# Three more expert matrices loaded in halves inside the attention, and five loaded ahead of the slots d0 to d4

## The chip, the cores and the metric

The kernel runs on one core of one Trainium2 chip. The engines are PE (matrix multiply, with its weight loads shown apart as PEld), DVE (vector), ACT (scalar), POOL (general purpose) and SP, which here does nothing but issue DMAs. The 16 DMA engines of the core carry every transfer, and the code of the engines too. The metric is the device time of one execution in microseconds (us).

## The reference

```python
# attention in chunks of 64 over q, k, v of shape (8, 8, 576, 64)
scores = scale * np.matmul(q_c, k_c.transpose(0, 1, 2, 4, 3))
attn = softmax(scores); out = np.matmul(attn, v_c)
x = out.transpose(0, 2, 1, 3).reshape(4608, 512)
# soft mixture of experts: 8 experts with 4 slots each
logits = x @ phi                                  # (4608, 32)
slot_input = softmax_over_tokens(logits).T @ x    # (32, 512)
h = np.maximum(slot_input[e] @ w1[e], 0.0)        # w1: 8 x 512 x 1024
slot_out[e] = h @ w2[e]                           # w2: 8 x 1024 x 512
x = softmax_over_slots(logits) @ slot_out         # (4608, 512)
# two-layer network
h = x @ w_in                                      # w_in: 512 x 2048
out = softplus(h) @ w_out                         # w_out: 2048 x 512
```

## The kernel before, in words

The work has three stretches. In the **attention** (about the first 175 us) 36 units, each of two heads and 512 tokens, go through the steps A (transposes of q and k on PE), B and M (copies on ACT and POOL), S (scores), m0, m1, x (softmax), C and Ce (transpose of P), D (times v), n0, n1 (normalise) and E; after every fourth unit the steps F add the unit's tokens to the slot inputs (`acc`). In the **transition** (about 175 to 240 us) PE multiplies the slot inputs with w1 in the sixteen steps H, one for each half of an expert's matrix, then with w2 in the sixteen steps SO, while the other engines prepare the combine weights (steps c1 to d) and split w_in and w_out into two parts (steps cb to cl). In the **network** (the rest) PE runs the two layers over tiles of 256 tokens.

All steps are put in order when the program is built: `issue` plays a list of steps with costs, ranks and buffers, and calls each step's function in the order that comes out. Every engine then runs its instructions in that order, and semaphores make an instruction wait for what it needs. SP issues all loads in order too. A load of q and k for unit u (step lq) waits until PE has finished the transposes of unit u - 3, because there are three buffers for raw q and k.

Each of w1 and w2 comes as sixteen matrices of 1 MB. `W1` and `W2` give the SBUF slot of each: the slots w0 to w7 hold a matrix as two halves, a and b, of 512 KB; g0 to g3, i0 to i3 and d0 to d4 hold it in one piece of 1 MB. The slots d0 to d4 lie where the attention keeps its buffers, so that these five loads wait for the last A (d0), the last S (d1, d2) and the last D (d3, d4). PE uses the w1 matrices in the order w0, w1, g0, g1, g2, d0 to d4, w2 to w6, g3, and the first five w2 matrices are those in i0 to i3 and w7. Two of the later SO steps have extra matmuls ahead of them that only fill time:

```python
FILL = {("SO", 14): 4, ("SO", 15): 3, ("o", 0): 2}
...
    ends = ((raw_ctx, "A1", ["d0"]), (qk_ctx, "S", ["d1", "d2"]), (v_ctx, "D", ["d3", "d4"]))
```

The functions that the change touches:

Of the kernel before, what the change touches and what calls it, by code (L numbers as in the profile page):

```python
# [17 lines left out]
LAG = 3  # L18
BUSY = 36
WAIT = 0  # L20
FILL = {("SO", 14): 4, ("SO", 15): 3, ("o", 0): 2}


# [2 lines left out]
W2 = ["i0", "i1", "i2", "i3", "w7", "w0", "w1", "w2", "w3", "w4", "w5", "w6", "g3", "i0", "i1",  # L26
      "i2"]
# [117 lines left out]
def kernel(  # L145
# [12 lines left out]
    nc = tc.nc  # L158
# [40 lines left out]
    wt = {}  # L199
# [11 lines left out]
    def slot(sl, dt=F32):  # L211
        return pools[home(sl)].tile([128, 2048], dt, tag=sl, name=sl)


    def half_slot(sl, i, dt=F32):
        nm = sl + "ab"[i]
        return pools[home(sl)].tile([128, 1024], dt, tag=nm, name=nm)

    def halves(sl):
        if sl[0] == "w":  # L220
            return [half_slot(sl, i) for i in range(2)]
        t = V["slot", sl] = slot(sl)
        return [t[:, 0:1024], t[:, 1024:2048]]
# [62 lines left out]
    def load(nm, n, sl):  # L286


        e, i = divmod(n, 2)
        if nm == "w1":  # L290
            src = moe_w1[e].rearrange("(p k) f -> p k f", k=4)[:, 2 * i:2 * i + 2]
        elif nm == "w2":
            src = moe_w2[e, i * 512:(i + 1) * 512, :].rearrange("(p b a) f -> p b (a f)", b=2, a=2)
        else:
            src = w_out_u[256 * n:256 * n + 256, :].rearrange("(k p) f -> p k f", p=128)
        parts = halves(sl)
        if sl[0] == "w":
            for t, x in zip(parts, (src[:, 0], src[:, 1])):
                nc.sync.dma_start(out=t.bitcast(U32) if nm == "wo" else t, in_=x)
        else:  # L300
            t = V["slot", sl]
            t = (t.bitcast(U32) if nm == "wo" else t).rearrange("p (b f) -> p b f", b=2)
            for x in (slice(0, 1), slice(1, 2)) if nm == "w2" and n >= 14 else (slice(0, 2),):
                nc.sync.dma_start(out=t[:, x], in_=src[:, x])
        if nm == "w2":
            parts = [t.rearrange("p (a f) -> p a f", a=2) for t in parts]
        wt[nm, n] = parts

    def load_wi(c, pr):
        src = w_in_u[256 * pr:256 * pr + 256, 1024 * c:1024 * c + 1024].rearrange(  # L310
            "(k p) f -> p k f", p=128)
        sl = WI[c][0][pr]
        parts = halves(sl)
        if sl[0] == "w":
            for i in range(2):
                nc.sync.dma_start(out=parts[i].bitcast(U32), in_=src[:, i])
        else:
            nc.sync.dma_start(
                out=V["slot", sl].bitcast(U32).rearrange("p (b f) -> p b f", b=2), in_=src)
        wt["wi", c, pr] = parts  # L320
# [297 lines left out]
    def add(nm, key, fn, deps=(), take=(), give=(), rank=0.0, cost=None, after=()):  # L618
        s = Step(nm, key, fn, [by[d] for d in deps if d in by], take, give, rank, cost,
                 [by[d] for d in after])  # L620
        by[nm, key] = s
        steps.append(s)

    for u in range(NU):
# [4 lines left out]
            cost={"SP": 2.4} if G == MIXED else None)  # L629
# [27 lines left out]
        n = HP - 1 if G == NG - 1 else 0  # L657
# [61 lines left out]
    def at(f, *a):  # L719
        return lambda e, held: f(*a)  # L720

    for n, sl in enumerate(W1):
        if sl[0] != "d":
            add("lw", ("w1", n), at(load, "w1", n, sl), rank=100 + n)
    for n in range(5):
        add("lw", ("w2", n), at(load, "w2", n, W2[n]), rank=130 + n)
    ends = ((raw_ctx, "A1", ["d0"]), (qk_ctx, "S", ["d1", "d2"]), (v_ctx, "D", ["d3", "d4"]))
    deps = []
    for i, (c, nm, sls) in enumerate(ends):
        add("close", i, at(lambda c, sls: (c.close(), [open_pool(sl) for sl in sls]), c, sls),  # L730
            deps + [(nm, k) for k in range(NU)])
        deps = [("close", i)]
        for sl in sls:
            n = W1.index(sl)
            add("lw", ("w1", n), at(load, "w1", n, sl), deps, rank=110 + n)
# [14 lines left out]
    for a in range(4):  # L750
        sl = slice(32 * a, 32 * a + 32)
# [3 lines left out]
    for a in range(4):  # L755
        sl = slice(32 * a, 32 * a + 32)
# [3 lines left out]
        out=phi, in_=moe_phi.rearrange("(k p) s -> p k s", p=128)), rank=2.5)  # L760
# [151 lines left out]
    def fill(key, t):  # L912
        for _ in range(FILL.get(key, 0)):
            nc.tensor.matmul(
                out=t[:, 0:256], lhsT=ident, rhs=acc[:, 0:256], start=True, stop=True)
# [277 lines left out]
    for nm, n in AFTER:  # L1193
        r += 1
        if nm == "wi":
            for pr in range(2):
                sl = WI[n][0][pr]
                k = ("wi", n, pr)
                add("lw", k, at(load_wi, n, pr), (), [(sl, ("wi", n))], (), r, {"SP": 2.65}, prev)
                prev = [("lw", k)]  # L1200
        else:
            sl = W2[n] if nm == "w2" else f"w{n}"
            add("lw", (nm, n), at(load, nm, n, sl), (), [(sl, nm + str(n))], (), r, None, prev)
            prev = [("lw", (nm, n))]
    for n in range(16):
        key = "w2" if n < 5 else f"w2{n}"
# [59 lines left out]
    for a, b in pieces[0]:  # L1266
        k = (0, a)
# [8 lines left out]
    for c in range(4):  # L1276
# [4 lines left out]
        n, d = need[c]  # L1281
# [21 lines left out]
    for n in range(NQ):  # L1303
# [6 lines left out]
        for i, p in enumerate(ps):  # L1310
            k = (n, p[0])
            f, l = i == 0, i == len(ps) - 1
# [56 lines left out]
    for s in steps:  # L1369
# [12 lines left out]
        if s.nm in ("cb0", "cx0") and s.key[:2] == ("wi", 1):  # L1382
            s.after = [*s.after, by["mx", (WAIT, 0)]]

# [31 lines left out]
```

## Time and profile before

| what | before |
|---|---|
| median of 3 runs | 679.87 us (679.12 to 679.99) |
| the profiled execution | 677.97 us, its span 676.2 us |
| PE busy | 634.6 us, 94% of the span |
| DVE, ACT, POOL busy | 430.2, 318.0, 237.8 us |
| DMA | 107.93 MB, mean 160 GB/s |

The span runs from the first to the last instruction that was recorded; 1.77 us of the execution lie outside it. A difference between two kernels is a difference of whole times. PE's busy share shows that whatever makes PE wait is the time to look for; a wait of another engine counts only where PE waits for it in turn.

### The profile page before, as it was taken

How to read it: one execution, taken by the hardware profiler on the slowest of the kernel's cores; microseconds unless marked ns; L12 is line 12 of the kernel's file. 1: busy time of each engine (PE TensorE's matmuls, PEld its weight loads, DVE VectorE, ACT ScalarE, POOL GpSimd, SP SyncE). 2: the span in 40 equal slices, each digit the busy share in tenths (PEclk: the TensorE clock that was granted, in tenths of full speed). 3: DMA queues.
4: the chain of work that ended last, by engine and by line, in shares of the span. 5: the costliest groups of instructions: out<-in, count | busy, mean ns of one | idle time of the engine just before them, and what ended most of it. 6: DMA issues, size and time to landing. Idle time of an engine off the chain costs nothing.

```text
span 676.2 us, 14087 instructions
## 1 busy us (share of the span) xinstructions
PE 634.6 (94%) x5849; PEld 511.6 (76%) x5849; DVE 430.2 (64%) x631; ACT 318.0 (47%) x478; POOL 237.8 (35%) x205
## 2 busy tenths in 40 slices
PE   5899899878995899999999999999999999999997
PEld 4688678756454677888788788888888888888885
DVE  1678778765237799878887877754555554545551
ACT  2566457543126587734554755544333333333330
POOL 4233233220114536613222233444433344433341
PEclk7999999998897999999999999999999999999999
DMA  9799889899999903112313510222414223231412
GB/s 169 195 245 275 234 235 287 212 300 413 416 409 411 391 5 128 59 63 93 125 63 118 195 62 32 79 78 79 110 62 125 63 85 103 78 110 63 121 35 62
DMA packets 80543, 107.93 MB, mean 160 GB/s; under 512 B 42464, under 2 KB 60896, under 8 KB 78560
## 3 DMA queue, kind: packets, MB, share of 16 engines
q1 hardware_dynamic: 80480, 107.04, 49.0%
q8 instruction: 46, 0.75, 0.5%
q14 instruction: 17, 0.14, 0.1%
HBM read 88.15 MB, written 18.87 MB: 158 GB/s over the span
## 4 chain that ended last, share of the span: by engine, by line
PE 81%; DVE 8%; issue 4%; ACT 3%; POOL 2%; DMA 1%; SPq 1%; POOLq 0%; DVEq 0%; ACTq 0%
PE trm L1146 18%; PE trm L1144 18%; PE trm L1142 18%; PE ph L1084 5%; PE tr L404 4%; PE X L487 3%; PE S L435 2%; PE hps L931 2%; PE tr L468 2%; PE tr L522 2%; PE tr L540 2%; PE tr L598 1%; DMA q<-in_q_dram 1%; DVE nm L446 1%; DVE ph L1113 1%
## 5 line engine op out<-in xcount | busy, mean ns | idle before, releaser
L1123 POOL TENSOR_TENSOR g<-hTm,g 128x1024 fp32r<-128x1024 f32 (+1 forms) x37 | 86.8, 2348 | 105.1 <-ACT g L1119 101.5
L1109 ACT ACTIVATE hTm<-hTm 128x1024 f32<-128x1024 f32 (+2 forms) x51 | 51.4, 1010 | 79.8 <-DVE hTm L1103 79.6
L1103 DVE TENSOR_SCALAR hTm<-ph 128x1024 uint32<-128x1024 uint32 (+2 forms) x51 | 59.0, 1158 | 34.6 <-PE ph L1084 34.5
L421 POOL COPY T<-T 64x512 f32<-64x512 f32 x72 | 44.0, 611 | 104.3 <-ACT T L413 103.5
L1113 DVE SCALAR_TENSOR_TENSOR hTm<-ph,hTm 128x1024 f32<-128x1024 f32 (+1 forms) x37 | 44.1, 1193 | 23.5 <-ACT hTm L1109 23.4
L1119 ACT CAST g<-hTm 128x1024 fp32r<-128x1024 f32 (+1 forms) x37 | 37.9, 1025 | 41.0 <-DVE hTm L1113 41.0
L1158 DVE TENSOR_TENSOR i<-trm,i 128x512 f32<-128x512 f32 x52 | 35.7, 686 | 32.0 <-PE trm L1146 31.8
L413 ACT COPY T<-tr 128x512 f32<-128x512 f32 x72 | 40.9, 588 | 29.5 <-PE tr L404 29.4
L1084 PEld LDWEIGHTS ph<-cT,Tc 128*128 128x128 f32 x288 | 43.6, 190 | 10.1 <-issue 2.8
L1084 PE MATMUL ph<-cT,Tc 128*128 128x256 f32 x288 | 47.0, 286 | 0.8 <-DVE ph L1113 0.7
L1103 DVE TENSOR_SCALAR siT<-ph 128x1024 uint32<-128x1024 uint32 (+1 forms) x25 | 29.5, 1180 | 26.0 <-PE ph L1084 26.0
L1123 POOL TENSOR_TENSOR g<-siT,g 128x1024 fp32r<-128x1024 f32 x12 | 28.9, 2407 | 42.8 <-ACT g L1119 42.8
L1109 ACT ACTIVATE siT<-siT 128x1024 f32<-128x1024 f32 (+1 forms) x25 | 25.7, 1026 | 36.8 <-DVE siT L1103 36.6
L1123 DVE TENSOR_TENSOR g<-ph,g 128x1024 fp32r<-128x1024 f32 (+2 forms) x27 | 29.7, 1102 | 11.9 <-ACT g L1119 11.9
L446 DVE TENSOR_REDUCE nm<-S 128x8 f32<-128x512 f32 x36 | 24.7, 686 | 18.9 <-PE S L435 18.8
L404 PE MATMUL tr<-ident,q 128*128 128x128 f32 x144 | 29.8, 290 | 6.3 <-DMA q<-in_q_dram 5.2
L1119 ACT CAST g<-ph 128x1024 fp32r<-128x1024 f32 (+2 forms) x27 | 24.9, 922 | 19.5 <-DVE ph L1113 18.1
L435 PEld LDWEIGHTS S<-T 64*64 64x64 f32 x1152 | 21.1, 137 | 16.1 <-issue 12.5
L435 PE MATMUL S<-T 64*64 64x64 f32 x1152 | 25.4, 225 | 7.5 <-issue 2.5
L404 PE MATMUL tr<-ident,k 128*128 128x128 f32 x144 | 28.9, 283 | 2.2 <-issue 2.2
L460 ACT ACTIVATE P<-P 128x512 f32<-128x512 f32 x36 | 23.0, 638 | 11.5 <-DVE P L452 11.4
L452 DVE TENSOR_TENSOR P<-S,nm 128x512 f32<-128x512 f32 x36 | 24.5, 679 | 2.1 <-PE S L435 1.3
(439 smaller groups left out, 1748.4 us busy)
## 6 DMA issues: line engine op xcount, KB each, us to landing
part<-i SPq DMA_DIRECT2D x18, 512.0 KB, 2.6
i<-part SPq DMA_DIRECT2D x18, 512.0 KB, 3.7
q<-in_q_dram SPq DMA_DIRECT2D x32, 256.0 KB, 4.7
k<-in_k_dram SPq DMA_DIRECT2D x32, 256.0 KB, 4.4
vbm<-in_v_dram SPq DMA_DIRECT2D x40, 128.0 KB, 4.2
g<-in_moe_w_dram SPq DMA_DIRECT2D x5, 1024.0 KB, 7.6
d<-in_moe_w_dram SPq DMA_DIRECT2D x5, 1024.0 KB, 12.1
i<-in_moe_w_dram SPq DMA_DIRECT2D x5, 1024.0 KB, 15.2
```

Of the source, the lines that this page charges most:

```text
L404: nc.tensor.transpose(c, t[:, h, 2 * rr:2 * rr + 2, :].rearrange("p r d -> p (r d)"), ident)
L421: nc.gpsimd.tensor_copy(out=t[a:a + 64, :, 1], in_=t[b:b + 64, :, 2 * h])
L435: nc.tensor.matmul(out=sp[64 * o:64 * o + 64, b, 64 * i:64 * i + 64], lhsT=cs[:, 0], rhs=cs[:, 1], start=True, stop=True)
L1084: nc.tensor.matmul(out=ph(n, a, b)[:, j - a, :], lhsT=K["Tc"][:, f * 128:(f + 1) * 128], rhs=K["cT"][:, t * TT:(t + 1) * TT], start=True, ...
L1103: nc.vector.tensor_scalar(out=scratch(n, a, b).bitcast(U32), in0=ph(n, a, b).bitcast(U32), scalar1=0x80000000, scalar2=None, op0=ALU.bitwi ...
L1109: nc.scalar.activation(out=y, in_=y, func=AF.Softplus)
L1113: nc.vector.scalar_tensor_tensor(out=soft(n, a, b), in0=ph(n, a, b), scalar=0.0, in1=y, op0=ALU.max, op1=ALU.add)
L1119: nc.scalar.copy(out=V["gs", n][:, 0, a:b], in_=soft(n, a, b))
L1123: tt(e)(out=s[:, 1, a:b], in0=soft(n, a, b), in1=s[:, 0, a:b].bitcast(F32), op=ALU.subtract)
L1142: nc.tensor.matmul(out=po, lhsT=s[:, 0, j, ts_], rhs=wr[:, hs], start=(n in begin and j == 0), stop=False)
L1144: nc.tensor.matmul(out=po, lhsT=s[:, 0, j, ts_], rhs=wr[:, ls], start=False, stop=False)
L1146: nc.tensor.matmul(out=po, lhsT=s[:, 1, j, ts_], rhs=wr[:, hs], start=False, stop=(j == 3 and n in finish))
```

## The change

Three w1 matrices, those of the slots w2, w3 and w4, no longer load after the last q and k. Each is loaded as two halves, and each half is issued straight behind q and k of one unit: units 8, 10, 12, 21, 26 and 31. The five w2 matrices of i0 to i3 and w7 are issued ahead of those of d0 to d4 instead of behind them. The steps that carried these loads stay in the list, with their cost and without their load, so that the planner's order for PE, DVE, ACT and POOL is what it was.

```diff
+EARLY_LOADS = {10: (8, 10), 11: (12, 21), 12: (26, 31)}
...
+    def load_half(n, sl, i):
+        src = moe_w1[n // 2].rearrange("(p k) f -> p k f", k=4)[:, 2 * (n % 2) + i]
+        if i == 0:
+            wt["w1", n] = halves(sl)
+        nc.sync.dma_start(out=wt["w1", n][i], in_=src)
+
...
+    def ahead(key, f, step):
+        add("ld", key, f, cost={None: 0.0}, after=[step])
+
     for n, sl in enumerate(W1):
         if sl[0] != "d":
-            add("lw", ("w1", n), at(load, "w1", n, sl), rank=100 + n)
+            add("lw", ("w1", n), at(lambda: None) if n in EARLY_LOADS else at(load, "w1", n, sl),
+                rank=100 + n)
+        for i, u in enumerate(EARLY_LOADS.get(n, ())):
+            ahead((n, i), at(load_half, n, sl, i), ("lq", u))
     for n in range(5):
-        add("lw", ("w2", n), at(load, "w2", n, W2[n]), rank=130 + n)
+        add("lw", ("w2", n), at(lambda: None), rank=130 + n)
+        ahead(("w2", n), at(load, "w2", n, W2[n]), ("lw", ("w1", 15)))
```

On SP, the first place is the loads of units 8 to 12. In the rows of before, q_586 and k_587 are those of unit 8, q_634 and k_635 of unit 9, and so on; vbm and vb2 take v, four DMAs for two units.

```order
L265 DMA q_586<-in_q_dram 128x2x256
L265 DMA k_587<-in_k_dram 128x2x256
L265 DMA q_634<-in_q_dram 128x2x256
L265 DMA k_635<-in_k_dram 128x2x256
L272 DMA vbm_115<-in_v_dram 128x4x64 x4
L265 DMA q_733<-in_q_dram 128x2x256
L265 DMA k_734<-in_k_dram 128x2x256
L265 DMA q_768<-in_q_dram 128x2x256
L265 DMA k_769<-in_k_dram 128x2x256
L272 DMA vb2_116<-in_v_dram 128x4x64 x4
```

The same place on SP in the changed kernel, whose lines stand one lower; L314 is the load of a half.

```order
L266 DMA q_586<-in_q_dram 128x2x256
L266 DMA k_587<-in_k_dram 128x2x256
L314 DMA w2a_590<-in_moe_w1_dram 128x1024
L266 DMA q_637<-in_q_dram 128x2x256
L266 DMA k_638<-in_k_dram 128x2x256
L273 DMA vbm_115<-in_v_dram 128x4x64 x4
L266 DMA q_736<-in_q_dram 128x2x256
L266 DMA k_737<-in_k_dram 128x2x256
L314 DMA w2b_591<-in_moe_w1_dram 128x1024
L266 DMA q_772<-in_q_dram 128x2x256
L266 DMA k_773<-in_k_dram 128x2x256
L273 DMA vb2_116<-in_v_dram 128x4x64 x4
```

Two halves have come between the loads of units 8 to 11; a third, w3a, follows behind unit 12.

The second place on SP is the loads of units 26 to 28 and the whole matrix g1 behind them, before the change.

```order
L265 DMA q_2103<-in_q_dram 128x2x256
L265 DMA k_2104<-in_k_dram 128x2x256
L265 DMA q_2135<-in_q_dram 128x2x256
L265 DMA k_2136<-in_k_dram 128x2x256
L272 DMA vbm_115<-in_v_dram 128x4x64 x4
L265 DMA q_2239<-in_q_dram 128x2x256
L265 DMA k_2240<-in_k_dram 128x2x256
L304 DMA g1_2271<-in_moe_w1_dram 128x2048
```

The same loads on SP after the change.

```order
L266 DMA q_2111<-in_q_dram 128x2x256
L266 DMA k_2112<-in_k_dram 128x2x256
L314 DMA w4a_2115<-in_moe_w1_dram 128x1024
L266 DMA q_2146<-in_q_dram 128x2x256
L266 DMA k_2147<-in_k_dram 128x2x256
L273 DMA vbm_115<-in_v_dram 128x4x64 x4
L266 DMA q_2250<-in_q_dram 128x2x256
L266 DMA k_2251<-in_k_dram 128x2x256
L305 DMA g1_2282<-in_moe_w1_dram 128x2048
```

The half w4a now stands behind unit 26, ahead of all that follows.

The third place on SP is the end of the attention, from the load of g3 on, before the change.

```order
L304 DMA g3_3235<-in_moe_w1_dram 128x2048
L304 DMA d0_3270<-in_moe_w1_dram 128x2048
L304 DMA d1_3287<-in_moe_w1_dram 128x2048
L304 DMA d2_3316<-in_moe_w1_dram 128x2048
L304 DMA d3_3324<-in_moe_w1_dram 128x2048
L304 DMA d4_3326<-in_moe_w1_dram 128x2048
L304 DMA i0_3328<-in_moe_w2_dram 128x2048
L304 DMA i1_3330<-in_moe_w2_dram 128x2048
L304 DMA i2_3332<-in_moe_w2_dram 128x2048
L304 DMA i3_3334<-in_moe_w2_dram 128x2048
L299 DMA w7a_3336<-in_moe_w2_dram 128x1024
L299 DMA w7b_3337<-in_moe_w2_dram 128x1024
```

The same stretch of SP after the change.

```order
L305 DMA g3_3235<-in_moe_w1_dram 128x2048
L305 DMA i0_3237<-in_moe_w2_dram 128x2048
L305 DMA i1_3239<-in_moe_w2_dram 128x2048
L305 DMA i2_3241<-in_moe_w2_dram 128x2048
L305 DMA i3_3243<-in_moe_w2_dram 128x2048
L300 DMA w7a_3245<-in_moe_w2_dram 128x1024
L300 DMA w7b_3246<-in_moe_w2_dram 128x1024
L305 DMA d0_3282<-in_moe_w1_dram 128x2048
L305 DMA d1_3299<-in_moe_w1_dram 128x2048
L305 DMA d2_3328<-in_moe_w1_dram 128x2048
L305 DMA d3_3336<-in_moe_w1_dram 128x2048
L305 DMA d4_3338<-in_moe_w1_dram 128x2048
```

The five w2 matrices have moved ahead of the five d slots. Ahead of g3 the loads of w2, w3 and w4 are gone, and those of w5 and w6 are left. On PE, DVE, ACT and POOL the rows are the same in both kernels.

## Rows read from the trace of the kernel before

**Rows 1.** The page's part 1: busy time of each engine, share of the span, instructions.

```profile
PE 634.6 (94%) x5849; PEld 511.6 (76%) x5849; DVE 430.2 (64%) x631; ACT 318.0 (47%) x478; POOL 237.8 (35%) x205
```

**Rows 2.** Stretches: us, busy PE, PEld, DVE, ACT, POOL (instructions), PEclk, DMA share, GB/s.

```profile
35.00:56.00 21.00, 20.55 (x544) 17.31 (x543) 15.81 (x37) 14.57 (x32) 7.95 (x13) 1.00 0.96 254
56.00:59.00 3.00, 3.00 (x31) 2.79 (x33) 2.84 (x9) 2.15 (x7) 0.74 (x2) 1.00 0.69 162
71.00:77.00 6.00, 6.00 (x116) 4.61 (x105) 4.94 (x15) 3.38 (x10) 1.22 (x2) 1.00 0.61 157
86.00:98.00 12.00, 11.36 (x276) 9.41 (x277) 9.65 (x21) 8.78 (x21) 4.28 (x7) 1.00 0.76 195
98.00:119.00 21.00, 19.98 (x546) 17.04 (x536) 17.85 (x41) 13.31 (x28) 6.72 (x11) 1.00 1.04 299
131.00:134.00 3.00, 2.71 (x66) 2.14 (x67) 2.44 (x5) 2.47 (x5) 1.65 (x4) 1.00 0.69 139
153.00:156.00 3.00, 3.00 (x60) 2.46 (x62) 2.12 (x5) 1.15 (x3) 0.61 (x1) 0.50 1.03 410
168.00:231.00 63.00, 53.28 (x538) 30.96 (x538) 29.87 (x57) 22.81 (x42) 19.77 (x13) 0.92 1.02 411
```

**Rows 3.** PE in order of time, pauses that nothing released: start, us, what, [idle before].

```profile
63.08 0.38 PE L404 MATMUL tr<-ident,q 128*128 128x128 f32 x2 [1.03 <-issue]
...
82.86 0.27 PE L404 MATMUL tr<-ident,k 128*128 128x128 f32 x1 [2.18 <-issue]
...
120.63 0.64 PE L540 MATMUL tr<-xT,phi 128*32 128x128 f32 x16 [1.40 <-issue]
...
143.33 0.34 PE L487 MATMUL X<-vbm,P 64*64 64x65 f32 x7 [1.70 <-issue]
...
151.59 0.33 PE L435 MATMUL S<-T 64*64 64x64 f32 x5 [2.49 <-issue]
...
158.00 0.56 PE L487 MATMUL X<-vbm,P 64*64 64x65 f32 x19 [0.59 <-issue]
...
167.33 0.73 PE L540 MATMUL tr<-xT,phi 128*32 128x128 f32 x17 [1.66 <-issue]
```

**Rows 4.** DMA queue of code: whole span, then 118.1 to 119.2: packets, MB, share.

```profile
q8 instruction: 46, 0.75, 0.5%
...
q8 instruction: 1, 0.02, 6.0%
```

**Rows 5.** k of unit 15: issue on SP, time to landing (last), first use on PE.

```profile
58.46 0.42 SPq L265 DMA_DIRECT2D k<-in_k_dram  x1
...
k<-in_k_dram SPq DMA_DIRECT2D x1, 256.0 KB, 5.2
...
64.61 0.38 PE L404 MATMUL tr<-ident,k 128*128 128x128 f32 x2
```

**Rows 6.** PE in order of time: two waits for DVE in the attention.

```profile
50.69 0.33 PE L435 MATMUL S<-T 64*64 64x64 f32 x6 [0.28 <-DVE P L452]
...
69.64 0.35 PE L435 MATMUL S<-T 64*64 64x64 f32 x9 [0.43 <-DVE P L452]
```

**Rows 7.** Landing of d4 (issued at 165.17), and PE's first H that reads d0.

```profile
d<-in_moe_w_dram SPq DMA_DIRECT2D x1, 1024.0 KB, 11.8
...
182.76 4.46 PE L931 MATMUL hps<-d,siT 128*32 128x512 f32 x40
```

**Rows 8.** Transition: a wait of PE; last w2 half, issue and landing; its step SO.

```profile
213.20 1.12 PE L850 MATMUL trm<-ident,cr 128*128 128x128 f32 x4 [4.72 <-POOL cr L843]
...
212.49 0.33 SPq L304 DMA_DIRECT2D i<-in_moe_w_dram  x1
...
i<-in_moe_w_dram SPq DMA_DIRECT2D x1, 512.0 KB, 12.7
...
224.23 1.56 PE L914 MATMUL hps<-acc,ident 128*128 128x256 f32 x6
225.72 1.08 PE L973 MATMUL sops<-i,hTm 128*32 128x256 f32 x16
```

## The prediction

> **What bounds the kernel now.** Read the page first: PE is busy for 634.6 of the 676.2 us of the span [rows 1], so a gain has to come out of the 41.6 us in which PE does nothing, and a loss is whatever adds to them. Next, the table of stretches [rows 2]. It shows two regimes of the DMA engines. In the attention they are nearly full but move only 250 to 300 GB/s (share 0.96 from 35 to 56 us, 1.04 from 98 to 119), with short gaps between (0.69, 0.61, 0.76). From 168 to 231 us they are full and move 411 GB/s. The change takes 3 MB out of the second regime and puts them into the first. So there are two questions: does PE wait for DMA in the transition, where loads get earlier, and is there room in the attention, where loads are added?
>
> For the first, look at PE's waits in the transition [rows 8]. The large one, 4.72 us before 213.20, ends with a POOL instruction, the split of combine weights, in which no load has a part. The last step SO starts at 225.72 behind 1.56 us of fill matmuls, and the last half of w2 was issued at 212.49 and took 12.7 us, so it landed at 225.2. The load is half a microsecond early: PE does not wait for it there, it runs the fill.
>
> For the second, look at the pauses of PE that nothing released [rows 3]. There are four in the attention up to 143 us (1.03, 2.18, 1.40 and 1.70, together 6.3 us) and three more up to 167 (2.49, 0.59, 1.66, together 4.7). They fall in the middle of a group of equal matmuls, so they aren't waits for data. PE has 2 x 5849 instructions [rows 1], and the queue that carries code has 46 packets of 16 KB [rows 4]: 254 instructions to a packet. One packet is in flight between 118.1 and 119.2 us [rows 4], and the pause that ends at 120.63 ends 1.4 us later. So I read these pauses as PE waiting for its own code, whose packet shares the 16 engines with the loads.
>
> **The change, step by step.** The sum is made against the profiled execution, 677.97 us, which is 1.90 below the median of the runs. A half of 512 KB costs the engines 0.524 MB / 411 GB/s = 1.28 us [rows 2], six halves 7.7 us. No row of before shows a half behind a unit's q and k, so its price for PE is bounded by nothing (all in gaps) and 1.28 us each (no gap). SP's own issue is under half a microsecond [rows 5, 8] and is free, since SP waits for PE to give buffers back.
>
> *w2a, w2b, w3a (behind units 8, 10, 12).* They add 3.84 us to the queue within some 14 us. The gaps up to unit 15 are 0.04 x 21 = 0.84 and 0.31 x 3 = 0.93 [rows 2], so 2.07 us are left over. k of unit 15 is issued at 58.46, lands 5.2 us later at 63.66, and is used at 64.61 [rows 5]: its margin is 0.95. As data it comes 1.12 us late. The code packet behind the pause at 63.08 has no margin at all (it is 1.03 us late already [rows 3]), and if it stands behind the whole queue the pause grows by the full 2.07. The two waits overlap, so the larger counts: between 1.1 and 2.1, I take the middle, **+1.6**.
>
> *w3b (behind unit 21, about 84 us).* The next gaps, 0.24 x 12 = 2.9 us up to 98 [rows 2], take all of it: **0**. Without that cover it would be 1.28.
>
> *w4a (behind unit 26, about 105 us).* From 98 to 119 there is no gap (1.04). All loads behind it, g1 among them, move back by 1.28, and so does the code packet of the 1.40 us pause [rows 3]: **+1.3**, at the upper bound, because this stretch is the fullest one.
>
> *w4b (behind unit 31, about 124 us).* The gap of 0.31 x 3 = 0.93 us at 131 to 134 takes most of it; 0.35 is left for the pause before 143.33 [rows 2, 3]: **+0.3**.
>
> *Given back.* Where PE has just been held, DVE is ahead, and two waits for DVE, 0.28 and 0.43 us [rows 6], that lie behind these places go: **-0.7**.
>
> *Five w2 matrices ahead of d0 to d4.* Their cost is a later d4. Before, 11 MB stand in the queue from w2 to d4; after, 13 MB from w5 to d4. At 1.05 MB / 411 GB/s = 2.55 us for a matrix that is 5.1 us later. d4 was issued at 165.17 and landed 11.8 later, at 177.0 [rows 7]; it now lands at 182.1. PE reads d0 from 182.76 and takes 4.46 us for the five d matrices [rows 7], 0.89 each, so it needs d4 at about 186.3; d0 lands four matrices (10.2 us) before d4. The margin is 4 us: **0**. If the cover went, each further microsecond would stall H one for one. SP also stops waiting between the d loads, but the engines are full there with or without that.
>
> *Transition.* The stream that ends with the last w2 half is 7.7 us shorter, so this half lands near 217.5 instead of 225.2. PE still has to come through the POOL wait at 213.20, the SO steps and both groups of fill, which the change leaves in. Only what switching from the fill to a waiting half could cost is gained: **-0.1**. The 7.7 us are slack, not time.
>
> Sum: 1.6 + 0 + 1.3 + 0.3 - 0.7 - 0.1 = +2.4 us, 680.4 on the scale of the profiled execution, and **682.3** on that of the median, 0.35% slower. A second estimate from the same rows: four pauses of 6.3 us in a stretch into which the kernel before loads five matrices (w0, w1, g0 to g2) are 1.26 us for 1 MB, 3.8 us for three more. That is the upper part of this forecast, whose own range is 680.5 to 684.5.
>
> A rule of the Trainium skill speaks against the pauses. Its page "Runtime: NRT & Kernel Launch", section "Instruction fetch mechanics", has each engine stream its code in blocks of 16 KB, 256 instructions, and calls the cost of crossing a block "mostly hidden". The size agrees with this trace (254 for a packet); that it is hidden doesn't, with 11.1 us of pauses between 63 and 168 us. If it held, the pauses would not grow and only the late data would count.
>
> **The rivals.**
>
> *No change.* The code packets slip between the loads, and pauses do not grow. What remains is 1.1 for late data, less 0.7 and 0.1: +0.3, 680.2. For it: pauses come only at some of the packets (seven of 46 [rows 3, 4]), and halves are shorter than the 1 MB matrices. Against it: with full engines packets do come late, and 98 to 119 has no gap. The rule above would lead here.
>
> *Faster: pauses vanish behind the attention.* Between 143 and 168 us three pauses cost 4.7 us, and behind the first the granted clock is 0.50, the lower level (1.2 GHz), for the 3 us from 153 to 156 [rows 2], which costs 1.5 more: 6.2 in all. The changed queue holds other matrices there: g3 and i0 to i3 with 8 KB to a partition, where before it was w2 to w6 with 4 KB. If a code packet gets in between these sooner, PE gains up to 6.2, and with the +2.4 from the attention the time is 679.87 + 2.4 - 6.2 = 676.1. It decides once more than 3.8 of the 6.2 us go. For it: from 168 to 231 the engines are full with matrices of both kinds and the list shows no such pause. Against: PE runs 538 matmuls in those 63 us [rows 2], so it seldom asks for code, and the first two packets after 143 still stand behind halves w5a to w6b.
>
> *Much slower: those pauses grow.* The same packets behind pieces of 1 MB (2.55 us) instead of 512 KB (1.28) come 1.28 later each, three times 3.8: 679.87 + 2.4 + 3.8 = 686.1. For it: the last two of the three packets would stand behind whole matrices where they stood behind halves. Against: the same as above.
>
> **How the numbers follow.** The forecast gets 0.45, no change 0.23, faster 0.20, much slower 0.12. A measurement here can tell 0.2% (1.4 us) from nothing. Slower by more than that: 0.42 from the forecast (its low end is within 0.2%) and 0.11 from the much slower case, 0.53. Same: 0.20 from no change, 0.03 from the forecast and 0.01 from the much slower case, 0.24. Faster: 0.20, and 0.03 from no change, which has a spread too, 0.23. The range runs from 677.0, which leaves out about half of the faster case, to 685.5, which leaves out most of the much slower one: 677.0 to 685.5 holds about 8 in 10.
>
> **What the profile would show.** Right: more pauses without a releaser on PE between 40 and 65 us and before 120 us, the end of the attention (the first H) some 2 us later, DMA engines that go idle before 225 us, the same 4.7 us wait for POOL ahead of the last combine transposes, and fill matmuls ahead of SO 14 and 15 with their data long there. Wrong: an attention as long as before, which would mean that the gaps take the halves; H waiting for a d matrix; or a transition shorter by microseconds, which would mean that some step in it did hang on a load and that I misread its releaser. The forecast fails most easily on the pauses: they depend on which load a code packet happens to stand behind, and every load after unit 8 is displaced.

## The result, and the profile after

The change makes the kernel slower. The median of 20 runs is 686.95 us (679.78 to 692.10) beside 676.73 us (674.43 to 681.16) for 20 runs of the kernel before on the same chip: a ratio of 1.0130, 95% interval 1.0106 to 1.0154, or 8.8 us [7.2, 10.4]. The ratio leaves out runs that took over 1.5% longer than the fastest of the same kernel, three of the changed kernel's 20, and the medians, which are 10.2 us apart, do not. (Where us stand for a ratio below, they are the ratio less 1 times the median of before.) The three runs of the kernel before that were known ahead of the prediction are in the upper half of its 20.

The profiled execution of the changed kernel took 679.78 us and is the fastest of the 20. It shows what the change does at its best, and it is not the run to read the size from; for that, two kernels with the same loads in the attention are used below. Page of after, part 1:

```profile
PE 637.6 (94%) x5849; PEld 512.5 (76%) x5849; DVE 429.3 (63%) x631; ACT 318.1 (47%) x478; POOL 238.1 (35%) x205
```

PE has the same 5849 matmuls as in [rows 1]. Its busy time is 3.0 us longer; work at a lower clock counts as busy too (56 to 59 us below: busy for all 3.00 us at a granted clock of 0.50). The stretches of after (us, busy PE, PEld, DVE, ACT, POOL, PEclk, DMA share, GB/s):

```profile
35.00:56.00 21.00, 18.47 (x445) 14.75 (x442) 13.74 (x29) 13.46 (x28) 6.74 (x11) 0.99 0.99 275
56.00:59.00 3.00, 3.00 (x80) 2.52 (x80) 1.67 (x6) 0.67 (x4) 0.61 (x1) 0.50 1.02 237
...
98.00:119.00 21.00, 17.25 (x410) 14.39 (x409) 14.43 (x34) 11.13 (x24) 5.68 (x11) 1.00 1.02 290
131.00:134.00 3.00, 2.96 (x109) 2.68 (x102) 2.47 (x6) 0.96 (x2) 0.15 (x1) 1.00 0.99 262
153.00:156.00 3.00, 2.79 (x65) 2.49 (x68) 2.24 (x5) 1.60 (x3) 0.61 (x1) 1.00 1.02 371
168.00:231.00 63.00, 53.86 (x592) 31.84 (x591) 29.47 (x59) 21.53 (x39) 18.61 (x12) 0.94 1.02 407
```

The gaps of the DMA engines at 56 to 59 and 131 to 134 us are full now (0.69 before, 1.02 and 0.99 now), and from 35 to 56 us PE runs 445 matmuls where it ran 544 [rows 2]. PE of after in order of time, the waits and pauses that matter, then the first H that reads a d slot and the last three steps SO:

```profile
54.33 0.41 PE L411 MATMUL tr<-ident,q 128*128 128x128 f32 x2 [2.19 <-DMA q<-in_q_dram]
...
107.89 0.52 PE L547 MATMUL tr<-xT,phi 128*32 128x128 f32 x9 [1.90 <-issue]
...
113.77 0.33 PE L529 MATMUL tr<-ident,x 128*128 128x128 f32 x1 [1.16 <-issue]
...
153.21 0.34 PE L442 MATMUL S<-T 64*64 64x64 f32 x5 [1.39 <-issue]
...
159.83 0.56 PE L494 MATMUL X<-vbm,P 64*64 64x65 f32 x19 [2.34 <-issue]
...
185.35 4.46 PE L945 MATMUL hps<-d,siT 128*32 128x512 f32 x40
...
215.78 2.59 PE L864 MATMUL trm<-ident,cr 128*128 128x128 f32 x12 [4.71 <-POOL cr L857]
...
226.28 1.56 PE L928 MATMUL hps<-acc,ident 128*128 128x256 f32 x6
227.77 1.08 PE L987 MATMUL sops<-i,hTm 128*32 128x256 f32 x16
```

Even in this run the first H on d0 stands at 185.35 instead of 182.76 [rows 7], 2.6 us later. The largest loss stands ahead of unit 13: q of unit 12, behind the halves w2a and w2b, comes 2.19 us late at 54.33, and the granted clock is 0.50, the lower of its two levels, in the 3 us from 56. The transition is half a microsecond shorter: 42.4 us from that H to the last SO, 42.96 before [rows 7, 8], with the same wait of 4.7 us for POOL in it. The loads that the change was to bring forward, on SP of after (the last d matrix and the last half of w2, issue and then time to landing):

```profile
169.76 0.42 SPq L305 DMA_DIRECT2D d<-in_moe_w_dram  x1
...
209.80 0.33 SPq L305 DMA_DIRECT2D i<-in_moe_w_dram  x1
...
d<-in_moe_w_dram SPq DMA_DIRECT2D x1, 1024.0 KB, 16.7
...
i<-in_moe_w_dram SPq DMA_DIRECT2D x1, 512.0 KB, 12.6
```

The last half lands at 222.4 and its SO starts at 227.77 behind the fill: 5.4 us of slack, where it was half a microsecond [rows 8]. The gain is there as slack, and nothing turns it into time.

### The profile page after: what moved, and what is told of

The parts are those of the page before. It is cut to its first block, busy times and chain, and to the rows that moved or that the text cites. A ratio compares the mean times of both kernels' runs of the same rounds, so it can differ in the third digit from the quotient of the medians.

```text
span 678.0 us, 14091 instructions
## 1 busy us (share of the span) xinstructions
PE 637.6 (94%) x5849; PEld 512.5 (76%) x5849; DVE 429.3 (63%) x631; ACT 318.1 (47%) x478; POOL 238.1 (35%) x205
## 4 chain that ended last, share of the span: by engine, by line
PE 80%; DMA 8%; DVE 7%; issue 2%; ACT 1%; SPq 1%; POOL 1%; DVEq 0%; POOLq 0%
PE trm L1160 18%; PE trm L1158 18%; PE trm L1156 18%; PE ph L1098 5%; PE tr L411 4%; PE X L494 3%; PE S L442 3%; PE tr L475 2%; PE tr L529 2%; DMA i<-in_moe_w_dram 2%; PE hps L945 2%; PE tr L547 2%; DMA w1b<-in_moe_w_out_dram 2%; PE tr L605 1%; DMA w3b<-in_moe_w_dram 1%
## 5 line engine op out<-in xcount | busy, mean ns | idle before, releaser
L1098 PEld LDWEIGHTS ph<-cT,Tc 128*128 128x128 f32 x288 | 43.6, 190 | 10.3 <-issue 2.8
L1133 ACT CAST g<-ph 128x1024 fp32r<-128x1024 f32 (+2 forms) x27 | 24.9, 921 | 19.5 <-DVE ph L1127 18.1
L529 PE MATMUL tr<-ident,x 128*128 128x128 f32 x144 | 23.6, 286 | 2.4 <-issue 1.3
```

Source lines behind the costliest of these rows:

```text
L1098: nc.tensor.matmul(out=ph(n, a, b)[:, j - a, :], lhsT=K["Tc"][:, f * 128:(f + 1) * 128], rhs=K["cT"][:, t * TT:(t + 1) * TT], start=True, ...
L1133: nc.scalar.copy(out=V["gs", n][:, 0, a:b], in_=soft(n, a, b))
```

## The experiments

The theory: in the attention the queue is full, so a half behind a unit's q and k makes loads and code packets late, and PE pays; the transition does not hang on loads. Rivals: the new order of the w2 and d matrices is what costs; the fill ahead of the last SO steps eats a gain that is there; or it is the 3 MB as such, wherever they stand. Where a short diff says "base", the change's second part (w2 ahead of d) is undone, so that only `EARLY_LOADS` differs from the kernel before. Each ratio is taken against runs of the kernel before on the same chip.

**The change again, and its two parts.** `again` is the changed kernel; `halves_only` is the base with all six halves; `reorder_only` has the new order of w2 and d alone; `first_matrix` is the base with w2a and w2b alone.

```diff
 # halves_only
-        add("lw", ("w2", n), at(lambda: None), rank=130 + n)
-        ahead(("w2", n), at(load, "w2", n, W2[n]), ("lw", ("w1", 15)))
+        add("lw", ("w2", n), at(load, "w2", n, W2[n]), rank=130 + n)
 # reorder_only
+EARLY_LOADS = {}
 # first_matrix, on the base
+EARLY_LOADS = {10: (8, 10)}
```

> The changed kernel a second time, for a second profile beside new timed runs, since its first profile (679.8 us) is the fastest of its 20 runs (median 687.0). Queue theory (the six halves overfill the DMA engines in the attention, so that loads of q, k and code come late there): 683 to 692 us, and a profile near 687 shows the first step H some 8 us or more after before's 176.8 us, with several waits of PE for q or k. Late-d theory (d0 to d4 behind five w2 matrices hold up H): the same time, but the attention as long as in the first profile and waits between the H steps of 3 to 8 us.

> Six halves early as in the changed kernel; the five w2 matrices stay behind d0 to d4 as before. Queue theory: keeps nearly all of the loss, 1.009 to 1.014 of before. Late-d theory: loses little, 1.000 to 1.004.

> Only the five w2 matrices go ahead of d0 to d4; the three w1 matrices stay behind the last q and k as before. Queue theory: 0.998 to 1.003 if d4 still comes in time. But here 16 MB stand ahead of d4 instead of 13, which is 7.7 us later than in the changed kernel, so d4 lands about 192 us where PE needs it at 186: some 5 us of waits in H in any case, about 1.007. Late-d theory: 1.008 to 1.02.

> Only the matrix of slot w2 goes early, its halves behind units 8 and 10; all else as before. Queue theory: a third of the bytes in the stretch with the least margin, 1.003 to 1.008. Late-d theory, and a theory that one matrix fits the gaps: 0.998 to 1.002.

Measured: `again` 1.0189 [1.0149, 1.0229], `halves_only` 1.0138 [1.0095, 1.0180], `reorder_only` 1.0103 [1.0067, 1.0139], `first_matrix` 1.0106 [1.0074, 1.0138]. The profiled execution of `again` took 905.14 us and is not read. The halves alone cost about what the whole change does, and one matrix out of three already three quarters of it. `halves_only` on PE, in order of time:

```profile
43.88 0.58 PE L442 MATMUL S<-T 64*64 64x64 f32 x24 [0.73 <-issue]
...
53.23 0.62 PE L442 MATMUL S<-T 64*64 64x64 f32 x26 [3.20 <-issue]
...
65.14 0.33 PE L411 MATMUL tr<-ident,q 128*128 128x128 f32 x1 [1.87 <-issue]
...
91.44 0.94 PE L442 MATMUL S<-T 64*64 64x64 f32 x32 [2.75 <-issue]
...
193.54 4.47 PE L944 MATMUL hps<-d,siT 128*32 128x512 f32 x40
...
237.09 1.15 PE L986 MATMUL sops<-i,hTm 128*32 128x256 f32 x16
```

Three pauses of 5.8 us fall between 43 and 66 us, where the kernel before has one of 1.03 us [rows 3], and d0 is read 10.8 us later than in [rows 7]; from there to the last SO (237.09) it is 43.6 us, 42.96 before. This execution took 688.89 us, which is near the usual time of the changed kernel. The new order costs by itself, where the prediction had put it at nothing, but in another situation: with no halves taken out, 16 MB stand from w2 to d4. PE of `reorder_only`, then the issue of its last d matrix and its time to landing:

```profile
186.01 1.07 PE L945 MATMUL hps<-d,siT 128*32 128x512 f32 x8 [0.73 <-DMA d<-in_moe_w_dram]
188.54 1.07 PE L945 MATMUL hps<-d,siT 128*32 128x512 f32 x8 [1.46 <-DMA d<-in_moe_w_dram]
```

```profile
170.49 0.33 SPq L305 DMA_DIRECT2D d<-in_moe_w_dram  x1
...
d<-in_moe_w_dram SPq DMA_DIRECT2D x1, 1024.0 KB, 18.0
```

H waits 2.2 us for the last two d matrices; d4 lands at 188.5. In after it lands at 186.4 and is needed at 185.35 + 4 x 0.89 = 188.9, so there it is not waited for. Of the 7 us that `reorder_only` lost in its runs, this profile shows 2.2; it is the fastest of its runs, and the rest stays open. So does how much the order adds to the whole change: the two parts alone, 1.38% and 1.03%, are more together than `again` or the first measurement of the change.

**Is the measurement steady, and do place and g1 matter?** `null` is the kernel before; `last_matrix`, `gap_matrix` are the base with one matrix each; in `late_g1` no half moves, and the 1 MB matrix g1 goes behind unit 35 instead of unit 28.

```diff
 # last_matrix
+EARLY_LOADS = {12: (26, 31)}
 # gap_matrix
+EARLY_LOADS = {10: (6, 18)}
 # late_g1
+LATE_LOADS = {3: 35}
...
+        if n in LATE_LOADS:
+            ahead(("late", n), at(load, "w1", n, sl), ("lq", LATE_LOADS[n]))
```

> The kernel before, unchanged, timed as if it were a change. Both the queue theory and the late-d theory: ratio 0.997 to 1.003. If it comes out near 1.01, then some 7 us of every difference measured so far lie in how the runs are taken and not in the kernels.

> Only the matrix of slot w4 goes early, its halves behind units 26 and 31. Queue theory: the loss follows the bytes in the attention wherever they go, so about what the halves behind units 8 and 10 cost (1.0106): 1.007 to 1.013. Theory of thin margins (the loss comes from the loads of units 10 to 12, which had under 2.5 us to spare): 1.001 to 1.005, since the loads behind w4a and w4b had 2.5 us and more.

> The matrix of slot w2 goes early, with its halves behind units 6 and 18, just where the DMA engines had gaps (share 0.31 from 26 to 29 us, 0.46 from 71 to 74). Queue theory with gaps: 0.999 to 1.004. If placing does not matter and any load added to the attention costs the same: 1.008 to 1.013.

> The opposite: the whole matrix g1, which before loads inside the attention behind unit 28, goes behind q and k of unit 35; all else as before. Queue theory: the attention gets 2 to 6 us shorter, the transition waits some 2 us for the last w2 half, which lands 2.6 us later (225.2 to 227.8, its step SO starts at 225.7): 0.993 to 1.000. Late-d theory: d0 to d4 land 2.6 us later with 10 us to spare: 1.000 to 1.005.

Measured: `null` 1.0008 [0.9982, 1.0035], `last_matrix` 1.0040 [1.0014, 1.0065], `gap_matrix` 0.9998 [0.9971, 1.0025], `late_g1` 0.9990 [0.9965, 1.0015]. The matrix that cost 1.06% behind units 8 and 10 costs nothing behind 6 and 18, where the DMA engines have gaps. The expectation that the loss of `last_matrix` would follow the bytes (1.007 to 1.013) was wrong, that of thin margins held. In the profile of `late_g1`, its fastest run, the attention is some 4 us shorter, and part of this is lost again because the last steps SO, which come earlier, now do wait for their loads:

```profile
216.04 1.09 PE L989 MATMUL sops<-i,hTm 128*32 128x256 f32 x16 [1.42 <-DMA i<-in_moe_w_dram]
...
219.89 1.06 PE L989 MATMUL sops<-i,hTm 128*32 128x256 f32 x8 [0.83 <-DMA i<-in_moe_w_dram]
```

**Does the fill hide a gain, and do the bytes cost?** The two kernels `..._nofill` leave out the seven fill matmuls ahead of SO 14 and 15, whose result nothing reads; `three_gaps` moves the same 3 MB as the change, to other units; `gap_late` puts the matrix in the gaps and g1 late.

```diff
 # after_nofill, on the change; gap_nofill, on gap_matrix
-FILL = {("SO", 14): 4, ("SO", 15): 3, ("o", 0): 2}
+FILL = {("o", 0): 2}
 # three_gaps, on the base
+EARLY_LOADS = {10: (6, 7), 11: (18, 23), 12: (5, 30)}
 # gap_late, on the base
+EARLY_LOADS = {10: (6, 18)}
+LATE_LOADS = {3: 35}
```

> The changed kernel without the fill matmuls ahead of SO 14 and SO 15 (it leaves out seven matmuls whose result nobody reads). Slack theory (the last w2 halves lie there 7 us early, PE only runs the fill): the stretch from the first H to the end of the last SO, 48.7 us in the changed kernel's profile, shrinks by about 3.2 us, and the time is 1.003 to 1.010 of before instead of 1.013 to 1.019. If the last SO steps do wait for loads, it shrinks by under 1 us. The attention is that of the changed kernel: the queue theory expects the first H between 182 and 192 us in a usual run.

> Halves of one matrix behind units 6 and 18, and no fill ahead of SO 14 and 15. Slack theory: the last w2 half lands 2.6 us earlier than in before (225.2 to about 222.6), the last SO can start at once, the stretch from H to SO shrinks by 2.5 to 3.3 us at no cost in the attention: 0.995 to 0.998. Rival (the fill is needed to keep the granted clock high): 0.999 to 1.003, with low clock behind 220 us.

> The same six halves as in the change, 3 MB, but behind units 6 and 7, 18 and 23, 5 and 30, where the stretches of before show gaps of the DMA engines; the w2 matrices stay where they were, the fill too. Queue theory with gaps: 0.999 to 1.005. Theory that the bytes alone count: as halves_only, 1.009 to 1.018.

> Two moves together: halves of the matrix of w2 behind units 6 and 18, and g1 behind unit 35. The number of bytes in the attention is that of before, only at other places. Queue theory: the pause ahead of 120 us goes and the transition does not get longer: 0.994 to 0.999. If bytes alone count: 1.000.

Measured: `after_nofill` 1.0167 [1.0127, 1.0208], `gap_nofill` 0.9997 [0.9970, 1.0024], `three_gaps` 0.9998 [0.9971, 1.0025], `gap_late` 0.9997 [0.9962, 1.0032]. The fill is not what eats the gain, and the bytes are not what costs: six halves in other places are free. Three expectations failed: that the time of `after_nofill` would fall to 1.003 to 1.010, and that `gap_nofill` and `gap_late` would be faster than before. No kernel of the study beats the one before by more than the measurement can tell. `three_gaps` on PE has small pauses until 143 us and reads d0 earlier than the kernel before (179.57, against 182.76):

```profile
86.60 0.46 PE L494 MATMUL X<-vb,P 64*64 64x65 f32 x15 [1.27 <-issue]
...
151.30 0.33 PE L442 MATMUL S<-T 64*64 64x64 f32 x4 [3.00 <-issue]
...
179.57 4.46 PE L944 MATMUL hps<-d,siT 128*32 128x512 f32 x40
```

(That run is the fastest of its kernel, so the 3 us are not a gain.) The profiled execution of `after_nofill` took 689.17 us, near its median of 688.15, and its attention is that of the changed kernel, load for load. PE in order of time:

```profile
50.40 0.76 PE L442 MATMUL S<-T 64*64 64x64 f32 x26 [2.37 <-issue]
...
62.09 0.33 PE L411 MATMUL tr<-ident,q 128*128 128x128 f32 x1 [1.61 <-issue]
...
76.36 0.38 PE L529 MATMUL tr<-ident,x 128*128 128x128 f32 x2 [3.17 <-issue]
...
90.50 0.69 PE L442 MATMUL S<-T 64*64 64x64 f32 x32 [2.47 <-issue]
96.97 0.46 PE L494 MATMUL X<-vb,P 64*64 64x65 f32 x15 [0.80 <-issue]
...
194.13 4.46 PE L945 MATMUL hps<-d,siT 128*32 128x512 f32 x40
...
237.45 1.17 PE L1006 MATMUL trm<-rep,ts 128*128 128x128 f32 x8 [3.52 <-DVE ts L997]
```

Here d0 is read 11.4 us later than in [rows 7]. From there to the end of the last SO, which is at 233.94, it takes 39.8 us where the kernel before takes 44.0 (225.72 + 1.08 - 182.76 [rows 7, 8]): leaving the fill out does bring the last SO forward, and then PE waits 3.52 us at 237.45 for a DVE step, where it waits 0.59 us in the kernel before and 1.26 in `gap_nofill`. That is the wait which would be next if the loads were ever the limit. Behind it the granted clock is at its lower level for 3.4 us (from 238.5); in `gap_nofill` it stays at the upper level behind 220 us, so there the rival of a clock held up by the fill falls. The pauses fall at the same instructions as in `halves_only`: the same 26 S matmuls, the same single transpose, the same 15 X. The code queue of `after_nofill` between 48 and 49 us:

```profile
q8 instruction: 1, 0.02, 6.1%
```

This packet starts at 48.02 and is through at 48.99; PE, which had stopped after 48.03, goes on at 50.40, 1.41 us after the packet's end. The stretches behind three of these pauses (columns as above):

```profile
50.00:54.00 4.00, 3.60 (x71) 3.15 (x71) 2.22 (x5) 0.59 (x1) 0.00 (x0) 0.59 0.93 229
76.00:80.00 4.00, 3.64 (x108) 3.14 (x108) 1.90 (x5) 2.29 (x5) 0.61 (x1) 1.00 0.68 175
91.00:95.00 4.00, 4.00 (x59) 3.46 (x48) 2.37 (x6) 1.30 (x4) 0.61 (x1) 0.59 1.05 282
```

Behind the first and the third the granted clock falls to the lower level (0.59 is the mean with a little of the full level in it), behind the longest not (1.00).

**Each half by itself.** Base kernels with one crowded half each, the other half behind unit 18, where it is free, and the matrix of units 12 and 21, with which all three are measured.

```diff
 # half_8, half_10, half_12, mid_matrix
+EARLY_LOADS = {10: (8, 18)}
+EARLY_LOADS = {10: (10, 18)}
+EARLY_LOADS = {11: (12, 18)}
+EARLY_LOADS = {11: (12, 21)}
```

> One half behind unit 8, the other behind unit 18, where the queue has a gap; the w2 matrices load as before. The pair behind units 8 and 10 cost 1.0106, the same matrix behind units 6 and 18 nothing (0.9998). Theory A, each half in the crowded stretch pays by itself: half of that, 1.004 to 1.007, with pauses of PE some 2 us longer between units 7 and 13. Theory B, the slack takes one half and the second is what costs: 0.998 to 1.002.

> One half behind unit 10, the other behind unit 18. Theory A: 1.004 to 1.007. Theory B: 0.998 to 1.002. If half_8 and half_10 come out far apart, it is the place, the loads and code packets that stand right behind the half, and not the amount, that sets the price.

> One half behind unit 12, the other behind unit 18, ahead of the only gap before unit 15. Theory A: 1.003 to 1.006, as for the halves behind units 8 and 10. Theory B: 0.998 to 1.002, as the one half is within the slack.

> The slot w3 alone, in halves behind units 12 and 21. The three matrices one by one were 1.0106 (units 8 and 10), 1.004 (units 26 and 31) and this; all three were 1.0138. If prices add, this is 1.0138 - 1.0106 - 1.004 + 2 = 0.999, so within 0.3% of no change. If it is slower by 0.4% or more, prices do not add: part of the pauses of one place is slack for the next. Theory A also wants the half behind unit 21 to show in the pause near 91 us: at least 1 us longer than in the kernel before.

Measured: `half_8` 1.0042 [1.0014, 1.0070], `half_10` 1.0078 [1.0046, 1.0110], `half_12` 1.0015 [0.9977, 1.0054], `mid_matrix` 1.0016 [0.9981, 1.0052]. The slack does not take the first half behind units 8 and 10 (theory B falls there; for unit 12 it fits as well), and the place matters: 2.8 us behind unit 8, 5.3 behind unit 10, 1.0 behind unit 12, the last within what can be told from nothing. The prices add within their intervals: 0.42 + 0.78 = 1.20% against 1.06% for the two together, and 1.06 + 0.16 + 0.40 = 1.62% for the three matrices against 1.38%. The half behind unit 21 adds nothing that can be told (`mid_matrix` less `half_12`), and the longer pause at 91 us that theory A wanted there is missing from the profile of `mid_matrix`, which has none over 0.3 us between 73 and 113 us that nothing released (its longest, 3.95 us, ends at 72.81). `half_10` on PE:

```profile
54.17 0.41 PE L411 MATMUL tr<-ident,q 128*128 128x128 f32 x2 [1.51 <-DMA q<-in_q_dram]
...
71.50 0.44 PE L529 MATMUL tr<-ident,x 128*128 128x128 f32 x2 [1.53 <-issue]
...
90.49 0.46 PE L494 MATMUL X<-vb,P 64*64 64x65 f32 x15 [2.91 <-issue]
...
178.26 1.92 PE L806 MATMUL trm<-rep4w,acc 128*128 128x32 f32 x8 [2.94 <-DVE rep4w L704]
```

The late q comes 13 us behind the half of unit 10 (issued at 41.21), the first pause 30 us; the pause at 90.49 stands behind the other half too, that of unit 18, and has its like in the kernel before in the 2.18 us at 82.86 [rows 3]. All pauses ahead of the first H that nothing released come to 9.5 us here and to 11.1 in the kernel before, so what `half_10` costs in this profile is not in their sum. d0 is read 4.9 us later (187.69); there are 1.8 us of waits for a late q, 6.8 us more at the lower clock between 150 and 185 us, which cost up to 3.4, and a wait for DVE at 178.26 that is 2.94 us and was 0.98 before; against them stand the pauses and a start of unit 7 that is 0.8 us earlier.

## Why the prediction was wrong in size

The direction and the main mechanism were right: slower, through code packets and unit loads that come late in an overfilled attention, with the gain of the transition left as slack. The time missed: +2.4 us forecast, +8.8 [7.2, 10.4] measured, above the top of the range. The profile of after looks closer, 679.78 us against 677.97 and d0 read 2.6 us later, but that is the luck of its fastest run, and it lacks the pauses between 40 and 65 us that the forecast wanted; one late q stands in their place.

**The step that failed** is the term of w2a, w2b and w3a, **+1.6**. By the kernels of one half each it is 2.8 + 5.3 + 1.0 = 9.1 us, or 7.2 [5.0, 9.4] for the first two measured together (`first_matrix`). Its first mistake is the bound: "its price for PE is bounded by nothing (all in gaps) and 1.28 us each (no gap)". The upper bound is no bound. `half_10` alone cost 5.3 us [3.1, 7.4], four times what the half takes from the engines. That no row of before has a half behind a unit's q and k was a matter of the rows that I picked: w0a and w0b are issued there at 59.95 and 60.47, behind q and k at 58.97 and 59.48, and I did not look at what they delay. I took the price to be the time by which the queue gets longer, paid once, at the first late load. Where the time goes is shown by the start of the units (the first transpose of each) in the kernel before and in `after_nofill`, with the pauses that nothing released and the time at the lower clock, all in us from the two traces:

```
units       before   after_nofill   longer   pauses before/after   low clock before/after
7 to 13      22.0       28.4         +6.4        0   / 4.5             0   / 3.4
13 to 21     34.6       39.4         +4.8        3.2 / 6.4             0   / 3.4
21 to 35     55.6       58.3         +2.7        3.1 / 4.6             0   / 0
35 to d0     35.2       33.9         -1.3        4.7 / 2.6             6.8 / 10.2
```

With 1.2 us by which unit 7 starts earlier this makes the 11.4 us. In the first row, 4.5 us of new pauses and 3.4 us at half the clock, which cost up to 1.7, are 6.2 of the 6.4 us. So two things were left out: there are three late packets in that row and not one, and the clock that falls behind some of them. I had counted the clock once, in a rival behind 143 us, and in no term of the attention. The place was wrong too. I looked for the first effect at unit 15, 24 us after the issue of w2a (34.40 in after); it comes at 41.88 and 50.40, and in the fast run of after as the late q of unit 12.

**Why the halves pay more than their own time.** Count PE's recorded matmuls and weight loads from the start. The pauses from 30 us to the first H that nothing released (0.3 us and longer) then stand at the same numbers in all kernels; five of them:

```
before        2194 2946 4706 5710 5962 6214 6468
halves_only   1192 1442 1946 2446 2948 3198 3956 4708 5208 5712 5962 6214
after_nofill  1192 1442 1946 2446 2948 3198 3956 4708 5208 5712 6214
half_10       2446 3198 3702 3954 4706 5710 5962
three_gaps     940 3198 3702 3956 5712 5964
```

They differ by multiples of 251, to within 5 (5276 from 1192 to 6468 is 21 times 251.2), near the 254 that I had worked out for a packet. So there is a crossing from one block of code to the next every 251 instructions, and a pause if the packet is not there. In `after_nofill` the packets start between 0.7 and 6.9 us after the crossing before, those of the long pauses (50.40, 76.36, 90.50) 6.1 to 6.9 us after it, and PE needs 4.5 to 6.6 us for a block in which it does not pause. The loads that are issued around the first of them take as long: w2b and the q, k and v behind it, issued from 42.3 to 47.0 us, 5.8 to 7.4 us, and w3a 6.5. I read this as a packet that is asked for at a crossing and then queues with the loads: while its wait and the 1.4 us behind it stay under the time of a block it costs nothing, and beyond that everything counts, at each crossing for as long as the queue is overfull. That a packet starts at once when nothing stands before it was not tried. The sentence of the Trainium skill, page "Runtime: NRT & Kernel Launch", section "Instruction fetch mechanics", that the next block is fetched while the current one runs agrees with these starts; that a crossing is mostly hidden does not, with 18.1 us of pauses ahead of H in `after_nofill`. My reading rests on `after_nofill` and `halves_only`, where these pauses come to 18.1 and 17.7 us (11.1 in the kernel before, 12.6 in `null`). For one half alone it is not shown: in `half_10` the pauses did not grow, and late loads, the clock and a wait for DVE stand in the profile instead.

**The other steps.** *w3b, 0:* right as far as it can be told; the half behind unit 21 adds 0.1 us, the difference of two kernels that are each known to some 2.4 us. *w4a and w4b, +1.3 and +0.3:* 2.7 us [1.0, 4.4] by `last_matrix`, within reach, but not in the place I gave: in its profile H starts only 1.1 us later, and 3 us go in the transition, where SO steps wait for their loads (0.76, 1.43 and 0.84 us), as in `late_g1`. They are late because the matrices that follow the last v start later: SP issues w2a at 149.78, in the kernel before at 143.76, and the last half of w2 lands at 230.1 instead of 225.2. In `late_g1` the SO steps come earlier and 1 MB more stands ahead of them. *Given back, -0.7:* not measured by itself. Both waits of [rows 6] are gone in after, `halves_only` and `after_nofill`, but in the last two a new wait of 0.48 us for DVE stands near 70 us; against a loss of 9 us this is nothing. *The w2 matrices ahead of d, 0:* for after the reason holds, since d4 is in time; but the margin is 2.5 us and not 4, and it lands at 186.4 and not 182.1, because the matrices that follow the last v start 4.6 us later (w5a at 148.39 in after, w2a at 143.76 before), and the DMA engines are full from there on. Whether the order costs something in the attention's last 30 us is open: `again` is 0.5% slower than `halves_only` on the same chip, with intervals that overlap. *Transition, -0.1:* right as far as a profile can tell: from the first H on d0 to the end of the span it is 492.7 us in after, 493.6 in `halves_only` and 493.4 before, so that the whole loss lies ahead of it. The slack is 5.4 us; the half lands at 222.4 and not at 217.5, again because the matrices start 4.6 us later.

**The second estimate** in the prediction, 1.26 us of pause for each 1 MB, 3.8 us for three, was nearer and still too small, for the same reason: pauses do not grow in proportion to the bytes. `three_gaps` moves the same bytes for nothing.

**The rivals.** *No change* and *faster* are refuted for these places. *Much slower* gave 686.1 on the scale of 679.87, a ratio of 1.009, and came nearest, by another mechanism: its pauses behind 143 us did not grow (4.7 us at the three places it names, 2.6 there in `after_nofill`), those between 40 and 100 did. One thing in the size can't be read from any single profile: the 17 runs of the changed kernel that the ratio uses spread over 10.0 us, those of the kernel before over 6.7, and the traces at hand are those of one run each.

## What to carry to other kernels

The price of a load in a stretch where the DMA engines are full is not its own time on them: it is paid at the instruction blocks and loads that come late behind it, and again where the granted clock falls. Here one half cost four times its own time behind unit 10, twice behind unit 8 and nothing clear of noise behind unit 12; so look for the next gap, and put the load right there (six halves in gaps: 0.9998, behind other units: 1.0138). If pauses of an engine without a releaser stand a fixed number of its instructions apart, as here, look at its code packets; every crossing without a pause has a margin that a new load can use up. Before a load is moved forward, ask what waits for it: here its new slack of 5 us was behind a POOL step and fill, and behind the fill a DVE step was next.

## What the hardware showed that I had not expected

- The pauses of PE in the attention that nothing released stand on a grid of 251 recorded instructions in every profile that was read, and PE goes on 1.1 to 1.6 us after the code packet is through.
- A code packet of 16 KB took 0.9 to 1.2 us itself, mostly, but started up to 6.9 us after the crossing before (`after_nofill`), as late as a load of 512 KB issued in that stretch lands (6.5 us).
- In `after_nofill` pauses of 2.4 us were followed by 3.4 us at the lower granted clock (the means 0.59 above), one of 3.2 us was not: such a stretch costs up to 1.7 us more, and the pause's length alone does not tell whether it comes.
